# A third pair of batch 2 in cluster order, and GpSimd's transfers tied to their slots

## The chip, the cores and the metric

The kernel runs on one core of a Trainium2 chip. The metric is device time in microseconds, the median of several executions; lower is better. Three executions of the kernel before took 944.02, 944.16 and 945.89 us, so its time is 944.16 us. The core's engines run side by side, each with its own instruction queue in order: TensorE (PE, matmuls), VectorE (DVE), ScalarE (ACT), GpSimd (POOL) and SyncE (SP, which here only starts transfers). They meet through semaphores.

## The reference, cut to what matters

Attention in which a query sees only the keys of its own cluster, and behind it a feed-forward network with a PReLU.

```python
# q, k, v: (4, 8, 768, 64); centroids: (8, 16, 64); scale = 1/8
q_assign = argmax(normalise(q) @ normalise(centroids).T)   # a cluster of 16 per query
k_assign = argmax(normalise(k) @ normalise(centroids).T)
scores = where(q_assign[..., None] == k_assign[..., None, :], scale * q @ k.T, -1e9)
attn = softmax(scores) @ v
x = attn.transpose(0, 2, 1, 3).reshape(3072, 512)
h = x @ w_in                                               # 512 x 2048
out = (maximum(h, 0) + alpha * minimum(h, 0)) @ w_out      # 2048 x 512
```

All inputs are random; all values are 32-bit floats.

## The kernel before

**Tiling.** The 8 heads of each of the 4 batches are taken two at a time: 16 *pairs*, four to a batch, numbered 0 to 15. A pair has 768 tokens, in six chunks of 128 keys. The feed-forward of a batch is done in two halves of 384 tokens, and each half consists of 28 *pieces*: 16 hidden ones (L1055, four matmuls, a copy out of PSUM on ScalarE at L1061, the PReLU's slope on VectorE at L1047) and 12 final ones (L1073, four matmuls; the result is copied by ScalarE at L1079 or added by VectorE at L1081, and stored by SyncE at L1084).

**Two ways to do a pair.** Pairs below `NO` (10 before) are done in two halves of 384 queries. Each half scores all six chunks of keys (L774), takes the exponentials on ScalarE (L795), masks them on VectorE by comparing clusters (`mask`, L815), adds them up (L825) and weighs the values (L929). Pairs from `NO` on are done *in cluster order*: the rows of q, k and v are first sorted by cluster, so that each chunk of keys scores only a window of queries (224, 384, 320, 320, 384 and 224 columns, 1856 of 4608 for a head), and the results are sorted back.

**What cluster order costs.** VectorE and a few small matmuls compute each row's rank (`order_sims` L572, the scan L586, `order_begins` L598, `order_rows`). Then 24 indirect transfers, started by GpSimd (`order_scatter`, L666), write the rows to a scratch tensor in DRAM. Four of them share one staging tile, which SyncE fills by three transfers (`order_stage`, L652), and GpSimd adds the row numbers to it (L663). There are two staging tiles. `order_load` (SyncE) fetches the sorted rows three or four steps ahead of the pair. After the attention, `weigh_near` (L962) and `normalise_near` make the result; `to_rows` turns it on TensorE (L992) and ScalarE copies it out (L995) into two tiles that every pair uses; twelve indirect transfers by GpSimd (`put_back`, L1000) write it to DRAM in the old order; `fetch_back` (SyncE, L1012) reads it and `turn_back` (VectorE, L1019) puts it into `xT`, the feed-forward's input.

**The order of the work** is written out by hand and the tile framework only adds the waits. The work is a list of *steps*, three to each half pair or whole pair, called a group. Before, batch 2 has steps 48 to 65: the whole pairs 10 and 11 at 48 and 51, then the first halves of 8 and 9 at 54 and 57, then their second halves at 60 and 63. Batch 3 is steps 66 to 77, four whole pairs. In the second part of the kernel, from step 24, a group has 15 *ticks*. The first three score the first three chunks, weigh and normalise the group before, and score the other chunks. The other twelve are *slots*. In each slot, in this order, one small task of the group runs, then up to one scatter (two in the slots of a group's first step) is taken from the deque `sorting` if it holds any, then feed-forward pieces are fed, so that a block's pieces are spread evenly over its slots. Things set by `later(k, ...)` run k ticks on: the put-backs of a pair run one per tick, from 8 to 19 ticks after its normalisation, `fetch_back` in the tick after them and `turn_back` nine ticks later.

The list `feeds` says from which step on a half of a batch is fed: the first half of batch 2 in steps 60 to 65, the second in 66 to 77, and `kept` says how many pieces are left over for the next block. `ORDERS` gives the step at which each sorted pair's loading starts.

**Waits.** Nothing holds GpSimd to its slot but the data: a scatter needs its staging tile and its ranks, a put-back its rows. SyncE is one queue in order, so a stage load that waits for scatters to free its tile holds all that is behind it, the stores and fetches too.

Of the kernel before, what the change touches and what calls it, by code (L numbers as in the profile page):

```python
# [10 lines left out]
FP32 = mybir.dt.float32  # L11
# [12 lines left out]
def kernel(  # L24
# [70 lines left out]
    def later(slots, piece):  # L95
        due.setdefault(now[0] + slots, []).append(piece)
# [5 lines left out]


    pairs = [(b, hp) for b in range(B) for hp in range(NCH)]
    NO = WHOLE * NCH - 2
    NP = len(pairs)
    raw_qk, vts = {}, {}

# [383 lines left out]
    def second_part():  # L492

        first_part.close()
        for name, bufs in (("emore", 1), ("ordc", 1), ("ordp", 1), ("order", NP - NO),
                           ("xmore", 1), ("byrow", 1)):
            sorts[name] = fast.enter_context(tc.tile_pool(name=name, bufs=bufs))
        for i in range(5):
            e_tiles.insert(0, sorts["emore"].tile([P, 2, HS], FP32, name=f"more{i}"))

    def order_constants():

        ordc = sorts["ordc"]
        stage = [ordc.tile([P, NX // PARTS, P], FP32, name=f"stage{i}") for i in range(STAGES)]
        place = ordc.tile([P, HS], U16, name="place")
        nc.gpsimd.iota(place, pattern=[[1, HS]], base=0, channel_multiplier=0)

        number = ordc.tile([P, NX], I32, name="number")
        nc.gpsimd.iota(number, pattern=[[TS, NX]], base=0, channel_multiplier=1)

        kinds = [[[0, P // NC], [1, NC]], [[2, 2], [0, 2], [1, 2], [0, NC]],
                 [[0, 2], [1, 2], [0, Q]]]
        rows, cols = [], ordc.tile([P, 3], FP32, name="cols")
        brief = asg.tile([P, HS], FP32, name="simT")
        assert NX // PARTS > len(kinds)
        own = stage[0][:, 0:len(kinds), :]
        for i, pattern in enumerate(kinds):
            row = (ordc.tile([P, P], FP32, name=f"row{i}") if i else brief[:, 0:P])
            nc.gpsimd.iota(row, pattern=pattern, base=0, channel_multiplier=0,
                           allow_small_or_imprecise_dtypes=True)  # L520
            nc.gpsimd.tensor_tensor(out=own[:, i, :], in0=row, in1=ident, op=ALU.mult)
            rows.append(row)
        same = brief[:, 2 * P:3 * P]
        before, within = rows[1], rows[2]
        shift = ordc.tile([P, 2], FP32, name="shift")

        def columns():
            nc.vector.tensor_reduce(out=cols, in_=own, axis=AX.X, op=ALU.add)
            for t in stage:
                nc.gpsimd.memset(t, 0.0)  # L530

        def sums_before():
            nc.vector.tensor_scalar(out=same, in0=rows[1], scalar1=cols[:, 1:2],
                                    scalar2=None, op0=ALU.is_equal)
            nc.vector.scalar_tensor_tensor(out=before, in0=rows[0], scalar=cols[:, 0:1],
                                           in1=same, op0=ALU.is_gt, op1=ALU.mult)

        def sums_within():  # L540
            nc.vector.scalar_tensor_tensor(out=same, in0=rows[0], scalar=cols[:, 0:1],
                                           in1=same, op0=ALU.is_equal, op1=ALU.mult)
            nc.vector.scalar_tensor_tensor(out=within, in0=rows[2], scalar=cols[:, 2:3],
                                           in1=same, op0=ALU.is_gt, op1=ALU.mult)
            nc.vector.tensor_tensor(out=within, in0=within, in1=before, op=ALU.add)

        def shifts():
            nc.vector.tensor_scalar(out=shift[:, 0:1], in0=cols[:, 2:3], scalar1=-float(HS),  # L550
                                    scalar2=None, op0=ALU.mult)
            nc.vector.tensor_scalar(out=shift[:, 1:2], in0=cols[:, 1:2], scalar1=2.0,
                                    scalar2=float(S), op0=ALU.is_ge, op1=ALU.mult)
            nc.vector.tensor_scalar(out=shift[:, 1:2], in0=shift[:, 1:2], scalar1=-1.0,
                                    scalar2=None, op0=ALU.add)
        for i, piece in enumerate((columns, sums_before, sums_within, shifts)):
            later(5 + i, piece)
        begins = ordc.tile([P, NP - NO], FP32, name="begins")
        sorts.update(stage=stage, number=number, place=place, before=before, within=within,
                     shift=shift, begins=begins)  # L560
# [71 lines left out]
    def order_clusters(n, begin):  # L632
# [9 lines left out]
            nc.vector.tensor_reduce(out=first, in_=begunT, axis=AX.X, op=ALU.add)  # L642
        firsts[n] = first

    def order_stage(n, i):

        b, hp = pairs[n]
        h, part = divmod(i, PARTS)
        head, t = 2 * hp + h, sorts["stage"][i % STAGES]
        rows = slice(part * S // PARTS, (part + 1) * S // PARTS)  # L650
        for src, p0, d0 in ((q, 0, 0), (k, TS, 0), (v, TS, D)):
            nc.sync.dma_start(out=t[p0:p0 + TS, :, d0:d0 + D],  # L652
                              in_=src[b, head, rows].rearrange("(x p) d -> p x d", p=TS))
# [18 lines left out]
    def order_load(n):  # L672
        assert len(scattered[n]) == 2 * NX
        whole = scratch.pop(n)[0]
        found = sorts["order"].tile([P, 2, NJ, 1], I32, name="found")
        for h in range(2):
            r0 = 2 * h * S
            nc.sync.dma_start(out=found[:, h], in_=whole.bitcast(I32)[
                r0:r0 + S, D:D + 1].rearrange("(j p) d -> p j d", p=P))
        orders[n] = found  # L680
        for w in range(2):
            raw = inp.tile([P, 2, NJ, D], FP32, name="qk")
            for h in range(2):
                r0 = (2 * h + w) * S
                for x in range(D // Q):
                    r = h * D + x * Q
                    nc.sync.dma_start(
                        out=raw.rearrange("p h j d -> p (h j d)")[r:r + Q, :].rearrange(
                            "p (t i) -> p t i", i=Q),
                        in_=whole[r0:r0 + S, x * Q:(x + 1) * Q].rearrange(  # L690
                            "(t p) i -> p t i", p=Q))
            raw_qk[n, w] = raw
        vt = vpool.tile([P, 2, NJ, D], FP32, name="vt")
        for h in range(2):
            r0 = (2 * h + 1) * S
            nc.sync.dma_start(out=vt[:, h], in_=whole[r0:r0 + S, D:2 * D].rearrange(
                "(j p) d -> p j d", p=P))
        vts[n] = vt
# [20 lines left out]
    for b in range(B):  # L719
        whole = [n for n in range(b * NCH, (b + 1) * NCH) if n >= NO]  # L720
        rest = [n for n in range(b * NCH, (b + 1) * NCH) if n < NO]
        begun_at.append(len(steps))
        steps += [(n, None, s) for n in whole for s in range(SB)]
        for half in range(2) if rest else ():
            if half:
                begun_at.append(len(steps))
            steps += [(n, half, s) for n in rest for s in range(SB)]
            feeds[len(steps)] = b, half
    begun_at.append(len(steps))
    assert NJ == 6 and GROUP == 2  # L730

# [265 lines left out]

    def put_back(to, place, rows, i):
        j, h = divmod(i, 2)
        nc.gpsimd.indirect_dma_start(  # L1000
            out=to[i],
            out_offset=bass.IndirectOffsetOnAxis(ap=place[:, h, j:j + 1], axis=0),
            in_=rows[j // HJ][:, j % HJ, h * D:(h + 1) * D], in_offset=None, element_offset=h * S * D)

    def fetch_back(n, whole):
# [11 lines left out]
        def turn_back():  # L1017
            for half in range(2):
                nc.vector.transpose(out=x_tile(b, half)[:, hp, :],  # L1019
                                    in_=raw[:, half * HS:(half + 1) * HS])  # L1020
        later(4 if n == NP - 1 else 9, turn_back)

    def x_tile(b, half):
        if (b, half) not in xTs:
# [330 lines left out]
    FREE = SLOTS * SB - 3  # L1355


    ORDERS = [26, 29, 35, 38, 41, 50]
    prep_at, load_at = {}, {}
    for (n, half), u in start_of.items():  # L1360
        def at(step, slot, piece):
            prep_at.setdefault((step, slot), []).append(piece)
        if half is None:
            t = ORDERS[n - NO]
            load_at.setdefault(t, []).append(lambda n=n: load(n))
            for i in range(2):
                at(t + 1, FIRST + i, lambda n=n, i=i: order_features(n, i))
            at(t + 2, 2, lambda n=n: order_sims(n))
            load_at.setdefault(u - (3 if n == NO + 1 else 4), []).append(
                lambda n=n: order_load(n))  # L1370
            at(u - 4, 0, lambda n=n: prep_clusters(n))
            for i in range(2):
# [42 lines left out]
    def feed_block(u):  # L1415
        if u == NS:

            for i, p in ((5, 0), (7, 1)):
                ffn[i] = lambda piece=ffn[i], p=p: (piece(), w_in_sums(p))
            ffn.extend(last_pieces())  # L1420
            return
        ffn.extend(ffn_pieces(*feeds[u]))

    def kept(u):


        return {NS: 12, begun_at[-2]: 8, begun_at[-3]: 2}.get(block_end(u), 0)

    def block_end(u):
        return min(x for x in begun_at if x > u)  # L1430
# [59 lines left out]
    for u in range(TOGETHER, NS + 1):  # L1490
# [54 lines left out]
        for i in slots:  # L1545
# [4 lines left out]
            places = (block_end(u) - block_start(u)) // SB * FREE  # L1550
            pieces = len(ffn) - kept(u) + -whole * (places - 1 - at_slot) // places
            todo.popleft()()
            room = 1 + (s == 0)
            while sorting and room:
                scatters, piece = sorting.popleft()
                piece()
# [229 lines left out]
```

## Time and profile before

| | |
|---|---|
| median of the runs | 944.16 us |
| profiled execution | 985.67 us, its span 983.8 us |
| mean granted TensorE clock in it | 0.982 |
| TensorE busy | 937.1 us, 95% |
| VectorE busy | 664.7 us, 68% |
| GpSimd busy | 286.1 us, 29% |
| ScalarE busy | 251.1 us, 26% |
| 144 scatters (L666) | 150.4 us, 1044 ns each |
| 72 put-backs (L1000) | 70.9 us, 985 ns each |

The profile is of one execution, and that one took longer than the timed ones. Busy time of an engine is the time in which it had at least one instruction under way; a group of rows of one line and form gives its count, busy time and mean duration, then the idle time just before its instructions and what ended most of it ("<-ACT rows L995": a result that line 995 wrote on ScalarE). Starting a transfer on GpSimd shows as a DMA_INDIRECT row; on SyncE (SPq) such rows are the queue's own. A matmul of 32-bit floats shows as two records.

### The profile page before, as it was taken

How to read it: one execution, taken by the hardware profiler on the slowest of the kernel's cores; microseconds unless marked ns; L12 is line 12 of the kernel's file. 1: busy time of each engine (PE TensorE's matmuls, PEld its weight loads, DVE VectorE, ACT ScalarE, POOL GpSimd, SP SyncE). 2: the span in 40 equal slices, each digit the busy share in tenths (PEclk: the TensorE clock that was granted, in tenths of full speed). 3: DMA queues.
4: the chain of work that ended last, by engine and by line, in shares of the span. 5: the costliest groups of instructions: out<-in, count | busy, mean ns of one | idle time of the engine just before them, and what ended most of it. 6: DMA issues, size and time to landing. Idle time of an engine off the chain costs nothing.

```text
span 983.8 us, 11365 instructions
## 1 busy us (share of the span) xinstructions
PE 937.1 (95%) x3995; PEld 502.6 (51%) x3995; DVE 664.7 (68%) x1247; ACT 251.1 (26%) x462; POOL 286.1 (29%) x333
## 2 busy tenths in 40 slices
PE   8999999999997999999994989999999999999997
PEld 5534444454453454444541544545455554556886
DVE  5897789799496677888970946554788636598200
ACT  5674534222121221221210312122222210221000
POOL 2332222110055266631376475000034351000000
PEclk9999999999998999999996899999999999999999
DMA  7442676064012455714822122902031112000000
GB/s 285 134 131 89 138 156 98 12 124 123 0 46 80 106 141 111 141 31 99 143 73 62 33 70 78 115 1 49 22 70 32 32 33 56 1 0 1 22 22 25
DMA packets 209665, 73.35 MB, mean 75 GB/s; under 512 B 194289, under 2 KB 198081, under 8 KB 209601
## 3 DMA queue, kind: packets, MB, share of 16 engines
q1 hardware_dynamic: 201840, 60.35, 28.7%
q0 software_dynamic: 6912, 11.81, 3.7%
q8 instruction: 33, 0.54, 0.2%
q10 hardware_dynamic: 848, 0.39, 0.2%
q14 instruction: 32, 0.25, 0.1%
HBM read 49.89 MB, written 22.28 MB: 73 GB/s over the span
## 4 chain that ended last, share of the span: by engine, by line
PE 85%; DVE 8%; another core or an unknown queue 3%; issue 2%; ACT 0%; DVEq 0%; POOL 0%; POOLq 0%; ACTq 0%
PE fps L1055 25%; PE fps L1073 23%; PE vps L929 7%; PE sps L774 6%; PE sps L1289 4%; PE sps L1233 4%; PE fps L774 3%; PE vps L1289 2%; PE vps L1233 2%; PE fps L1289 1%; PE fps L1233 1%; PE vps L962 1%; PE sps L783 1%; PE mps L962 1%
## 5 line engine op out<-in xcount | busy, mean ns | idle before, releaser
L1055 PE MATMUL fps<-xT,w_in_sb 128*128 128x384 f32 x768 | 260.2, 493 | 7.0 <-issue 5.5
L1073 PE MATMUL fps<-w_out_sb,gT 128*128 128x512 f32 x576 | 256.5, 599 | 4.7 <-issue 3.5
L666 POOL DMA_INDIRECT scratch<-stage,off x144 | 150.4, 1044 | 196.9 <-DVE acc L825 69.2
L1055 PEld LDWEIGHTS fps<-xT,w_in_sb 128*128 128x128 f32 x768 | 143.8, 191 | 111.0 <-issue 13.1
L1073 PEld LDWEIGHTS fps<-w_out_sb,gT 128*128 128x128 f32 x576 | 107.9, 191 | 138.8 <-issue 129.6
L1000 POOL DMA_INDIRECT back<-rows,found x72 | 70.9, 985 | 175.8 <-ACT rows L995 155.3
L1061 ACT COPY gT<-fps 128x384 f32<-128x384 f32 x96 | 46.0, 479 | 231.6 <-PE fps L1055 193.6
L1047 DVE SCALAR_TENSOR_TENSOR gT<-gT,alpha 128x384 f32<-128x384 f32 x96 | 61.1, 648 | 57.3 <-ACT gT L1061 43.1
L774 PE MATMUL sps<-qkT 64*128 64x384 f32 (+1 forms) x480 | 89.4, 487 | 0.0
L795 ACT ACTIVATE E<-sps 128x768 f32<-128x768 f32 (+1 forms) x78 | 58.1, 789 | 78.1 <-PE sps L783 38.4
L897 DVE RECIPROCAL inverses<-mps 64x12 f32<-64x12 f32 (+1 forms) x44 | 11.0, 249 | 82.2 <-remote 40.5
L774 PEld LDWEIGHTS sps<-qkT 64*128 64x128 f32 x480 | 43.5, 186 | 40.0 <-issue 14.8
L815 DVE SCALAR_TENSOR_TENSOR more<-aq,key,more 128x384 f32<-128x384 bf16 (+2 forms) x120 | 63.1, 585 | 1.3 <-ACT more L792 1.1
L929 PE MATMUL vps<-E,vt 128*64 128x384 f32 x316 | 58.6, 495 | 1.4 <-DVE xT L1031 1.4
L815 DVE SCALAR_TENSOR_TENSOR E<-aq,key,E 128x384 f32<-128x384 bf16 (+2 forms) x96 | 50.2, 577 | 3.8 <-ACT E L795 1.6
L825 DVE TENSOR_TENSOR acc<-acc,E 128x768 f32<-128x768 f32 x37 | 35.3, 954 | 14.7 <-ACT E L795 13.6
L271 POOL TENSOR_TENSOR w_in_sb<-w_in_sb,power 128x512 f32<-128x512 f32 x16 | 24.0, 1502 | 69.2 <-DVE w_in_sb L268 69.2
L795 ACT ACTIVATE more<-sps 128x768 f32<-128x768 f32 (+1 forms) x42 | 31.1, 774 | 37.2 <-PE sps L774 33.8
L271 POOL TENSOR_TENSOR w_out_sb<-w_out_sb,power 128x512 f32<-128x512 f32 x16 | 22.9, 1433 | 57.3 <-DVE w_out_sb L268 57.3
L1079 ACT COPY y<-fps 128x512 f32<-128x512 f32 x18 | 10.6, 586 | 105.7 <-PE fps L1073 82.6
L774 PE MATMUL fps<-qkT 64*128 64x384 f32 (+1 forms) x144 | 33.1, 497 | 3.1 <-ACT y L1079 2.9
L1081 DVE TENSOR_TENSOR y<-y,fps 128x512 f32<-128x512 f32 x24 | 16.4, 682 | 26.2 <-PE fps L1073 26.2
(281 smaller groups left out, 1118.9 us busy)
## 6 DMA issues: line engine op xcount, KB each, us to landing
raw<-in_moe_w_in_dram SPq DMA_DIRECT2D x16, 512.0 KB
raw<-in_moe_w_out_dram SPq DMA_DIRECT2D x16, 512.0 KB
out_dram<-y SPq DMA_DIRECT2D x21, 256.0 KB
qk<-in_q_dram SPq DMA_DIRECT2D x48, 96.0 KB
qk<-in_k_dram SPq DMA_DIRECT2D x48, 96.0 KB
qk<-scratch SPq DMA_DIRECT2D x48, 96.0 KB
w_in_kept<-w_in_sb SPq DMA_DIRECT2D x8, 512.0 KB
vt<-in_v_dram SPq DMA_DIRECT2D x10, 384.0 KB
```

The source lines that it names most:

```text
L271: nc.gpsimd.tensor_tensor(out=dst, in0=dst, in1=power[0].bitcast(FP32), op=ALU.mult)
L666: nc.gpsimd.indirect_dma_start(out=scratch[n][1][h * NX + xx], out_offset=bass.IndirectOffsetOnAxis(ap=ranks[n][:, xx, h:h + 1], axis=0), ...
L774: nc.tensor.matmul(out=bank(ps, h, m), lhsT=qkT[r:r + D, S + c * P:S + (c + 1) * P], rhs=qkT[r:r + D, tokens], start=True, stop=not early_ ...
L795: nc.scalar.activation(out=E[:, :, 0:m], in_=ps[:, :, 0:m], func=AF.Exp, scale=SCALE)
L815: nc.vector.scalar_tensor_tensor(out=e, in0=of, scalar=keys[n][:, NJ + c, h:h + 1], in1=e, op0=ALU.is_equal, op1=ALU.mult)
L929: nc.tensor.matmul(out=po[r:r + D, 0:HS], lhsT=vts[n][:, h, c, :], rhs=e[:, h, :], start=(c == 0), stop=(c == NJ - 1))
L1000: nc.gpsimd.indirect_dma_start(out=to[i], out_offset=bass.IndirectOffsetOnAxis(ap=place[:, h, j:j + 1], axis=0), in_=rows[j // HJ][:, j % ...
L1047: nc.vector.scalar_tensor_tensor(out=gs[f], in0=gs[f], scalar=alpha[:, f:f + 1], in1=gs[f], op0=ALU.mult, op1=ALU.max)
L1055: nc.tensor.matmul(out=ps[:, 0:HS], lhsT=w_in_sb[:, c, f * P:(f + 1) * P], rhs=xTs[b, half][:, c, :], start=(c == 0), stop=(c == NCH - 1))
L1073: nc.tensor.matmul(out=ps[:, 0:DM], lhsT=gs[f][:, i * P:(i + 1) * P], rhs=w_out_sb[:, f, :], start=on and f == f0, stop=off and f == f0 + ...
L1233: nc.tensor.matmul(out=bank[to], lhsT=w_in_form(m, x, cc), rhs=rhs[:, cc, :], start=start and cc == 0, stop=cc == KH - 1, skip_group_check ...
L1289: nc.tensor.matmul(out=bank[to], lhsT=g_form(m, x, t), rhs=w_out_form(n, x), start=start and x == 0, stop=x == NQ - 1, skip_group_check=no ...
```

## The change

`NO` becomes 9, so that pair 9 is done in cluster order too, and three of batch 2's four pairs are. Batch 2 now has steps 48 to 62: whole pairs 9, 10 and 11 at 48, 51 and 54, then both halves of pair 8 at 57 and 60. Batch 3 is steps 63 to 74, and there are 75 steps, not 78. Both feed-forward halves of batch 2 are fed from step 63 on, behind its attention; the slots of steps 48 to 62 get the pieces of the second half of batch 1.

GpSimd is tied to the slots: `pace()` has ScalarE write one number into a tile of one element and GpSimd copy that tile. It stands ahead of each put-back and in each slot that takes something from `sorting`. The pool has 8 such tiles.

Around it: the tile `found` (the sorted rows' old places) moves into the tile of the ranks, the pool "order" has one buffer more, `order_load` runs three steps ahead for three pairs and four for the others, `turn_back` comes seven ticks after the fetch, and steps from 45 on may take two scatters in one slot more of a group.

```diff
-    NO = WHOLE * NCH - 2
+    NO = WHOLE * NCH - 3
...
-                           ("xmore", 1), ("byrow", 1)):
+                           ("xmore", 1), ("byrow", 1), ("pace", 8)):
...
+        sorts["paced"] = ordc.tile([1, 1], FP32, name="paced")
...
+    def pace():
+
+        token = sorts["pace"].tile([1, 1], FP32, name="pace")
+        nc.scalar.copy(token, ones[0:1, 0:1])
+        nc.gpsimd.tensor_copy(out=sorts["paced"], in_=token)
+
     def order_stage(n, i):
...
-        found = sorts["order"].tile([P, 2, NJ, 1], I32, name="found")
+        found = ranks[n].rearrange("p x h -> p (x h)")[:, 0:2 * NJ].rearrange(
+            "p (h j d) -> p h j d", h=2, d=1)
...
-            if half:
+            if half and not whole:
                 begun_at.append(len(steps))
             steps += [(n, half, s) for n in rest for s in range(SB)]
-            feeds[len(steps)] = b, half
+            feeds[len(steps)] = [(b, 0), (b, 1)] if whole else [(b, half)]
...
     def put_back(to, place, rows, i):
         j, h = divmod(i, 2)
+        pace()
         nc.gpsimd.indirect_dma_start(
...
-        later(4 if n == NP - 1 else 9, turn_back)
+        later(4 if n == NP - 1 else 7, turn_back)
...
-    ORDERS = [26, 29, 35, 38, 41, 50]
+    ORDERS = [26, 29, 35, 38, 41, 53, 56]
...
-            load_at.setdefault(u - (3 if n == NO + 1 else 4), []).append(
+            load_at.setdefault(u - (3 if n in (NO + 1, NO + 2, NP - 1) else 4), []).append(
                 lambda n=n: order_load(n))
...
-        ffn.extend(ffn_pieces(*feeds[u]))
+        for b, half in feeds[u]:
+            ffn.extend(ffn_pieces(b, half))
...
-        return {NS: 12, begun_at[-2]: 8, begun_at[-3]: 2}.get(block_end(u), 0)
+        return {NS: 12, begun_at[-2]: 2, begun_at[-3]: 2}.get(block_end(u), 0)
...
-            room = 1 + (s == 0)
+            room = 1 + (s == 0 or (u >= NS - 30 and (s, i) == (1, 0)))
+            if room and sorting:
+                pace()
             while sorting and room:
```

## The prediction

> **What bounds the kernel now.** I read the busy times first, then the chain that ended last, the groups of GpSimd, the waits, and last the timeline around 550 to 607 us, where batch 2's two cluster-ordered pairs are put back while pairs of batch 3 are still scattered.
>
> ```profile
> PE 937.1 (95%) x3995; PEld 502.6 (51%) x3995; DVE 664.7 (68%) x1247; ACT 251.1 (26%) x462; POOL 286.1 (29%) x333
> PE 85%; DVE 8%; another core or an unknown queue 3%; issue 2%; ACT 0%; DVEq 0%; POOL 0%; POOLq 0%; ACTq 0%
> ```
>
> TensorE is the bound: busy 95%, with 85% of the chain. What shortens TensorE's work pays in full, unless something holds it up. ScalarE has room, and GpSimd looks idle on average. The average misleads: GpSimd's transfers are crowded into stretches. The groups of GpSimd (count, then busy us and mean ns, then idle before):
>
> ```profile
> L666 POOL DMA_INDIRECT scratch<-stage,off x144 | 150.4, 1044 | 196.9 <-DVE acc L825 69.2 <-DMA stage<-in_v_dram 62.7 <-issue 34.3
> L1000 POOL DMA_INDIRECT back<-rows,found x72 | 70.9, 985 | 175.8 <-ACT rows L995 155.3 <-issue 20.2 <-DMA stage<-in_q_dram 0.3
> L663 POOL COPY stage<-number 64x4 int32<-64x4 int32 x36 | 9.4, 262 | 0.0
> ```
>
> Now the timeline (start, duration, instruction, idle before it). The second half of a pair's rows is ready at 560.97 (first line), but its first put-back runs at 570.38, 9.4 us late, and GpSimd is back to back (0.30 idle) up to the last at 582.56:
>
> ```profile
> 560.49 0.48 ACT L995 COPY rows<-mps 128x384 f32<-128x384 f32 x1
> ...
> 567.42 1.04 POOL L1000 DMA_INDIRECT back<-rows,found  x1 [0.30 <-issue]
> 568.46 0.27 POOL L663 COPY stage<-number 64x4 int32<-64x4 int32 x1
> 569.01 1.06 POOL L666 DMA_INDIRECT scratch<-stage,off  x1 [0.28 <-issue]
> 570.38 0.96 POOL L1000 DMA_INDIRECT back<-rows,found  x1 [0.30 <-issue]
> ...
> 582.56 0.96 POOL L1000 DMA_INDIRECT back<-rows,found  x1 [0.30 <-issue]
> ...
> 606.54 0.98 POOL L666 DMA_INDIRECT scratch<-stage,off  x1 [7.01 <-DMA stage<-in_v_dram]
> ```
>
> So a scatter costs 1.044 + 0.30 = 1.34 us of GpSimd, a put-back 0.985 + 0.30 = 1.29. Here lateness costs TensorE nothing: the one thing that waits for put-backs at once, ScalarE's copy into the rows (L995), lost 3.3 us to them in the whole span.
>
> The profiled execution took 985.67 us, 41.5 over the median. It holds stalls in which TensorE, VectorE, ScalarE and SyncE stand together while GpSimd goes on; the largest is in the waits (us, times, longest):
>
> ```profile
> DVE inverses L897 <- remote: 40.5, 3, 29.9
> ...
> SPq L652 <- DMA scratch<-stage,off: 121.3, 15, 51.4
> ```
>
> These stalls add up to 40 to 47 us, about the whole excess, so I take them to belong to the profiled execution and not to the runs. My sum is a difference between kernels, made on the profile's durations outside the stalls and laid on the median.
>
> **What the Trainium skill says.** "DMA: Bandwidth & Descriptors", section SWDGE vs HWDGE vs iDMA: descriptors of a GpSimd DMA are computed in software on GpSimd itself; SyncE's are not. The trace agrees: each transfer holds GpSimd about 1 us. "SBUF — State Buffer", section A bandwidth-pool intuition that's wrong: such a DMA takes about 620 ns alone and about 3100 ns beside a VectorE copy that locks the shared port. Here the shortest is 0.96 us; the page gives me the ends of a transfer's price. "ScalarE: Activation LUTs", section What ACT_TABLE_LOAD costs: an ACTIVATE takes 186 ns + 0.833 ns per element; this trace's 128x1 ones take 202 and 203 ns.
>
> **The change, part by part.**
>
> (1) Pair 9 goes in cluster order. A half pair's TensorE groups, between 604 and 686 us: scores 5.3 us / 28 = 0.189 each, weighing (5.0 + 4.4) / 52 = 0.181. Two halves are 48 of each: 9.1 + 8.7 = 17.8, and 0.6 for folding sums. A whole pair scores 1856 of 4608 columns. By the spacing of starts its 24 narrower scores take 3.9 us, weighing 3.9, turning to rows 0.65, begins 0.5, sums 0.4, together 9.4; its similarities cost what the other form's do. Saving 18.4 − 9.4 = 9.0. The busy totals of the narrow groups, which count twice where two matmuls overlap, give a smaller saving, 6.5. Spacing is the better measure of what the engine has left for others, so I take **8.5**, with the ends 6.5 and 9.
>
> (2) Feed-forward order. No piece is added or removed: batch 2's two halves (28 pieces each, about 85 us a half) run behind its attention, 28 pieces over 60 slots in steps 48 to 62, then 46 over 48 slots in steps 63 to 74. TensorE's sum is unchanged. VectorE in steps 48 to 62 comes to 127 to 131 us (three ordered groups at 19.7, two half groups at 15.5, feed-forward 13, sorting and preparing the rest) beside 133 of TensorE: covered, with little left. If not covered: 3 to 5 us.
>
> (3) The token. Before each slot's scatters and each put-back, ScalarE writes one number and GpSimd copies it: about 228 tokens (144 slots, 84 put-backs). ScalarE 228 × 0.2 = 46 us on an engine busy 26%: hidden while ScalarE runs ahead of TensorE's need. GpSimd about 0.17 each (below the 0.26 of L663), 39 us. The token lies in a pool of 8 tiles, so ScalarE's token n waits until GpSimd has copied token n − 8. Behind that ScalarE instruction stand the exponentials and the feed-forward's copies out of PSUM, and TensorE waits for those banks. So **GpSimd may be at most eight tokens late before it stops ScalarE and then TensorE**; and it can no longer run scatters ahead of their slot, as it did 10 to 39 us before 553 us. That is new.
>
> (4) GpSimd's demand against TensorE's supply of time, counted from the code by step and slot (58.1 is step 58, slot 1). TensorE's side is the whole or half pair of (1) and the feed-forward pieces of these slots, at 8 × 36.8 / 112 = 2.6 us for a hidden piece (L1055) and 8 × 28.2 / 64 = 3.5 for a final one (L1073); GpSimd's side (12 put-backs per ordered pair from eight ticks after it is normalised; up to one scatter a slot, two in the slots of a group's first step):
> Steps 52.4 to 55.3: 12 put-backs (15.5) + 15 scatters (20.1) + 4 copies and 24 tokens (5.6) = 41 us, while TensorE's work there is 28.
> 55.4 to 58.0: 12 put-backs, 1 scatter, 13 tokens = 19 against 23.
> 58.1 to 62.4: 12 put-backs, 24 scatters, 6 copies, 33 tokens = 55 against 41.
> Together 116 against 92, excess 24. Further, pair 14's first stage loads are queued on SyncE behind pair 10's fetch back, in the same tick, which waits for the last put-back: from the timeline 1.6 + 2.8 + 1.9 + about 2.5 = 8.7 us of idle GpSimd. Against it eight tokens of lateness, about 8 × 1.5 = 12 us, are free. ScalarE's stall: 24 + (0 to 9) − 12 = 12 to 21; part of it falls where TensorE has feed-forward ends that VectorE adds up. I take **15**, bounds 0 (a transfer of about 1.0 us with its token, where demand meets supply) and 28.
>
> (5) Turning back 7 ticks after the fetch instead of 9. Fetches that come late make VectorE wait 3 to 7 us at step 56 and 62, mostly inside (4)'s stall: **1**, bounds 0 to 4. The positions kept in the ranks' tile, the later load by one step: SyncE's, off the path, 0 to 1.
>
> Sum: −8.5 + 15 + 1 = +7.5; 944.2 + 7.5 = 951.7, say **951**.
>
> **Rivals.**
> A. GpSimd keeps up, and ScalarE is never held. For it: GpSimd was 29% busy, and unprofiled transfers may be shorter than 1.04 (the page's 0.62). Against: 0.30 between transfers and the crowd at 553 to 583. It decides at a period below about 1.1 us, token included. Then 944.2 − 8.5 + 1 = **937**, faster (935 to 942).
> B. VectorE becomes the bound in steps 48 to 62: 129 of 133 busy, and groups of steps 57 to 59 need 31.7 of VectorE beside 27.6. Without (4): −8.5 + 4 = **940**, faster.
> C. The profile's stalls are in the runs too and the tokens take them away, by keeping GpSimd from running ahead: 944 − 8.5 − 10 or more, **925 to 930**. Against: median and profile differ by just their sum.
> D. The token stall is just as large as the gain: 942.5 to 946, no change, at a period near 1.2 us.
>
> **How the numbers follow.** A difference under 0.2% (1.9 us) is what a measurement of this kernel can't tell from none. Held by GpSimd: 0.57, own range 946.5 to 961. D: 0.07. A 0.20, B 0.13, C 0.03: faster 0.36. The range reaches from 936 (A and B nearly whole; below it lie C and A's best, 0.08) to 961 (15 + 9 of stall, above it 0.1).
>
> **What would show it.** Right: ScalarE rows of a 1x1 copy waiting for GpSimd in steps 52 to 63, TensorE gaps there of 12 us or more in sum, GpSimd back to back, and the group of weighing (L929) down by 48 records. Wrong: no ScalarE wait on GpSimd's copy, TensorE without gaps between steps 48 and 63; or a transfer period well under 1.2 us. If the runs held the profiled stalls, or if GpSimd's wait for a token cost more than 0.3 us each, my sum is wrong from its base.

## The result, and the profile after

The changed kernel takes 973.34 us (970.51 to 974.19), the kernel before beside it 945.02 us: a ratio of 1.0297, 95% interval 1.0279 to 1.0315. It is **slower by 28.3 us**, where +7.5 was forecast (951, range 936 to 961). The direction was right; the size was wrong by nearly four times.

The page of the changed kernel (busy time and share; then the chain that ended last; then groups with count, busy us and mean ns, and idle before). Its profiled execution took 972.51 us, like the others:

```profile
PE 928.9 (96%) x3963; PEld 499.2 (51%) x3963; DVE 658.5 (68%) x1246; ACT 267.0 (28%) x679; POOL 393.3 (41%) x598
...
PE 76%; POOL 8%; DVE 6%; issue 3%; DMA 3%; SPq 2%; ACT 1%; POOLq 0%; ACTq 0%; DVEq 0%
...
L673 POOL DMA_INDIRECT scratch<-stage,off x168 | 180.1, 1072 | 74.4 <-issue 30.7
...
L650 POOL COPY paced<-pace 1x1 f32<-1x1 f32 x223 | 59.1, 265 | 161.9 <-ACT pace L649 160.3
...
L1009 POOL DMA_INDIRECT back<-rows,off x84 | 87.3, 1039 | 19.9 <-issue 14.8
```

In the profile ahead of the prediction GpSimd had no part in the chain and TensorE had 85%; now GpSimd holds 8% and TensorE 76%. The waits of the changed kernel (us, times, longest) name the hold that the prediction expected:

```profile
POOL paced L650 <- ACT pace L649: 160.3, 31, 57.8
...
ACT pace L649 <- POOL paced L650: 69.5, 45, 5.6
...
DVE xT L1028 <- DMA qk<-back: 22.6, 3, 8.1
```

In the first line GpSimd waits for its slot, which is what the tokens are for. In the second ScalarE waits for GpSimd's copy of the token eight before, 69.5 us in 45 places, 41 of them between 481 and 606 us. The third is VectorE waiting in order for a fetch that comes late.

The profile before, as the prediction had it, held stops of all engines. So the kernel before was run again for a trace without them.

> The kernel before, unaltered, for a trace of it from the same chip. Theory 4 (GpSimd, not ScalarE's hold, is what batch 2 is bound by once a third pair is in cluster order; the wait that passes it on to TensorE is whichever comes first: the token, the rows' tiles, the fetch back): where it takes about 944 us, its trace has no stop of all engines, and TensorE's gaps between 20 and 900 us are under 12 us in sum.

It took 944.51 us (ratio 0.9997, 0.9989 to 1.0005). The profiled execution, 947.29 us with a span of 944.9, holds no stop, and its gaps between 20 and 900 us come to 9 us; it is the one to compare. Its page and chain, and then its window of 485 to 625 us (us; busy PE, PEld, DVE, ACT, POOL; granted TensorE clock; DMA share; GB/s):

```profile
PE 926.9 (98%) x3995; PEld 498.5 (53%) x3995; DVE 662.2 (70%) x1247; ACT 249.5 (26%) x462; POOL 298.1 (32%) x333
PE 88%; DVE 5%; DMA 2%; SPq 2%; issue 1%; POOL 1%; ACT 0%; DVEq 0%; POOLq 0%; ACTq 0%
```

```profile
485.00:625.00 140.00, 138.41 (x505) 69.07 (x504) 93.18 (x165) 31.10 (x60) 80.58 (x85) 0.99 0.35 73
```

The same view of the changed kernel, in stages and in one:

```profile
485.00:505.00 20.00, 14.80 (x49) 7.16 (x49) 9.79 (x19) 5.19 (x19) 15.63 (x27) 0.83 0.38 89
505.00:525.00 20.00, 12.83 (x60) 6.05 (x57) 15.35 (x32) 4.30 (x17) 15.91 (x27) 0.83 0.30 60
...
565.00:585.00 20.00, 11.98 (x50) 5.54 (x50) 11.23 (x23) 7.17 (x23) 17.82 (x29) 0.74 0.57 106
...
485.00:625.00 140.00, 113.48 (x429) 55.52 (x428) 93.60 (x178) 35.33 (x124) 107.96 (x172) 0.90 0.44 90
```

Read two things. TensorE stands for 140 − 113.5 = 26.5 us of this stretch, against 1.6 before: 25 us of new gaps. And while it is busy its granted clock is 0.90, not 0.99: 113.5 × 0.10 = 11.3 us of its busy time is lost to the clock, against 1.4, so 10 more. With 7 us of matmuls saved (below), −7 + 25 + 10 = +28, close to the measured 28.3 (the spans of these two profiled executions differ by 25.7, since the one before is a little above its median). The gaps and the slow clock lie in batch 2's block: outside it TensorE's idle time in the two kernels agrees within 1.3 us.

### The profile page after: what moved, and what is told of

It reads as the page before. It is cut to its first block, busy times and chain, and to the rows that moved or that the text cites. A ratio compares the mean times of both kernels' runs of the same rounds, so it can differ in the third digit from the quotient of the medians.

```text
span 970.6 us, 12039 instructions
## 1 busy us (share of the span) xinstructions
PE 928.9 (96%) x3963; PEld 499.2 (51%) x3963; DVE 658.5 (68%) x1246; ACT 267.0 (28%) x679; POOL 393.3 (41%) x598
## 4 chain that ended last, share of the span: by engine, by line
PE 76%; POOL 8%; DVE 6%; issue 3%; DMA 3%; SPq 2%; ACT 1%; POOLq 0%; ACTq 0%; DVEq 0%
PE fps L1082 22%; PE fps L1064 20%; PE vps L937 6%; PE sps L782 5%; PE sps L1298 4%; PE sps L1242 4%; POOL back L1009 3%; POOL scratch L673 3%; PE vps L1298 2%; PE vps L1242 2%; PE fps L782 2%; POOL paced L650 2%; PE fps L1242 1%; PE fps L1298 1%; DMA stage<-in_v_dram 1%
## 5 line engine op out<-in xcount | busy, mean ns | idle before, releaser
L673 POOL DMA_INDIRECT scratch<-stage,off x168 | 180.1, 1072 | 74.4 <-issue 30.7
L650 POOL COPY paced<-pace 1x1 f32<-1x1 f32 x223 | 59.1, 265 | 161.9 <-ACT pace L649 160.3
L1009 POOL DMA_INDIRECT back<-rows,off x84 | 87.3, 1039 | 19.9 <-issue 14.8
L782 PE MATMUL sps<-qkT 64*128 64x384 f32 (+1 forms) x464 | 85.7, 485 | 0.0
L803 ACT ACTIVATE E<-sps 128x768 f32<-128x768 f32 (+1 forms) x76 | 56.1, 785 | 59.2 <-PE sps L791 39.0
L823 DVE SCALAR_TENSOR_TENSOR more<-aq,key,more 128x384 f32<-128x384 bf16 (+2 forms) x116 | 60.7, 580 | 1.3 <-ACT more L800 0.8
L937 PE MATMUL vps<-E,vt 128*64 128x384 f32 x292 | 54.6, 498 | 1.4 <-DVE xT L1040 1.4
L649 ACT COPY pace<-ones 1x1 f32<-1x1 f32 x223 | 33.6, 185 | 69.6 <-POOL paced L650 69.5
L271 POOL TENSOR_TENSOR w_in_sb<-w_in_sb,power 128x512 f32<-128x512 f32 x16 | 23.7, 1482 | 69.5 <-DVE w_in_sb L268 69.5
L823 DVE SCALAR_TENSOR_TENSOR E<-aq,key,E 128x384 f32<-128x384 bf16 (+2 forms) x88 | 45.3, 570 | 0.7 <-ACT E L800 0.6
L833 DVE TENSOR_TENSOR acc<-acc,E 128x768 f32<-128x768 f32 x35 | 33.3, 951 | 14.6 <-ACT E L803 13.6
```

What stands on the lines that cost most here:

```text
L650: nc.gpsimd.tensor_copy(out=sorts["paced"], in_=token)
L673: nc.gpsimd.indirect_dma_start(out=scratch[n][1][h * NX + xx], out_offset=bass.IndirectOffsetOnAxis(ap=ranks[n][:, xx, h:h + 1], axis=0), ...
L782: nc.tensor.matmul(out=bank(ps, h, m), lhsT=qkT[r:r + D, S + c * P:S + (c + 1) * P], rhs=qkT[r:r + D, tokens], start=True, stop=not early_ ...
L803: nc.scalar.activation(out=E[:, :, 0:m], in_=ps[:, :, 0:m], func=AF.Exp, scale=SCALE)
L823: nc.vector.scalar_tensor_tensor(out=e, in0=of, scalar=keys[n][:, NJ + c, h:h + 1], in1=e, op0=ALU.is_equal, op1=ALU.mult)
L937: nc.tensor.matmul(out=po[r:r + D, 0:HS], lhsT=vts[n][:, h, c, :], rhs=e[:, h, :], start=(c == 0), stop=(c == NJ - 1))
```

## The experiments

The theories are these. *1*: the window of eight tokens stops ScalarE and so TensorE, as forecast. *2*: GpSimd's lateness reaches TensorE anyway, by rows that are free late and fetches that come late. *3*: the tokens' own instructions, and that GpSimd may no longer run ahead, cost most. *4*, formed after the first results and a sharper form of 2: once a third pair is in cluster order GpSimd bounds batch 2's block, and whichever wait comes first passes that on.

The kernel before was measured beside each run and took 944.1 to 945.0 us. In three sets it took 998 to 1012 us, because there the other engines stop now and then while GpSimd sends; those six runs (the first five and the last in order of time) are kept apart, under "Where the engines stop".

**No tokens.** The two calls of `pace()` are left out; nothing holds GpSimd to its slot.

```diff
-        pace()
         nc.gpsimd.indirect_dma_start(
...
-            if room and sorting:
-                pace()
```

> The changed kernel without tokens, again, since the chips differ. Where the kernel before takes about 944 us (no stop of the other engines beside GpSimd's bursts), theory 1 gives 934 to 940 us: the third pair alone is worth its matmuls, and the tokens cost the rest. Where the kernel before takes 990 us or more, the other engines stop beside GpSimd's bursts, and with 12 more put-backs and 24 more scatters it is 10 to 30 us slower than before.

953.63 us beside 944.62, ratio 1.0091 (1.0075 to 1.0108). Without a token the kernel is still 9 us slower than before, where 934 to 940 was expected, so theory 1 is not the whole cause. But taking all tokens away does win 973.3 − 953.6 = 19.7 us; the next two runs divide that. In the timeline of this run ScalarE waits again, for something else:

```profile
512.50 0.48 ACT L1003 COPY rows<-mps 128x384 f32<-128x384 f32 x1 [11.42 <-DMA back<-rows,off]
```

The put-backs of the pair before still read the rows' tile, and the copy into that tile stands for 11.4 us. TensorE has a gap of 8.9 us behind it.

**A window of 128 tokens.** One tile of 128 numbers in turn replaces the pool of 8 tiles.

```diff
-        token = sorts["pace"].tile([1, 1], FP32, name="pace")
+        token = sorts["tokens"][:, i:i + 1]      # i counts up, modulo 128
```

> The changed kernel with 128 tokens, again. Where the kernel before takes about 944 us, theory 1 gives 936 to 944 us (ScalarE is never held by GpSimd's copy). Where it takes 990 us or more, the time is within 6 us of the changed kernel's, 984 us: without the hold, GpSimd falls behind and then runs back to back, and the other engines stop beside it instead.

966.77 us beside 944.62, ratio 1.0223 (1.0203 to 1.0244): 6.6 us below the changed kernel, not 30. The hold at eight is real but small, and theory 1 falls as the main cause: once it is gone, ScalarE waits 16.6 us for the rows' tile instead.

**GpSimd's copy alone**, read from a constant, with no number of ScalarE's.

```diff
-        token = sorts["pace"].tile([1, 1], FP32, name="pace")
-        nc.scalar.copy(token, ones[0:1, 0:1])
-        nc.gpsimd.tensor_copy(out=sorts["paced"], in_=token)
+        nc.gpsimd.tensor_copy(out=sorts["paced"], in_=ones[0:1, 0:1])
```

> The changed kernel with GpSimd's copy kept in each place but read from a constant, so that no number of ScalarE's is waited for and nothing holds ScalarE. It parts the 13 us between no tokens (953.6 us) and a window of 128 tokens (966.8 us). If GpSimd's copies cost it by their own time (223 at 0.04 to 0.2 us more a transfer): 960 to 967 us where the kernel before takes about 944. If the loss is that GpSimd may not run ahead of the slot: 953 to 957 us.

962.71 us beside 944.82, ratio 1.0195. GpSimd's copies cost 962.7 − 953.6 = 9.1 us, writing the slot's number on ScalarE and waiting for it 966.8 − 962.7 = 4.1, the hold at eight 973.3 − 966.8 = 6.5. These are the steps in this one order; in another they could divide otherwise. So theory 3 holds for the larger part of what the tokens cost, though not for the whole loss. A copy takes the place of most of the pause between two transfers, as GpSimd's timeline of the changed kernel shows (a scatter, the copy, the next scatter: 1.31 us from start to start, against 1.26 without a copy), so most copies add little more than 0.05 us:

```profile
495.25 0.97 POOL L673 DMA_INDIRECT scratch<-stage,off  x1 [0.16 <-issue]
496.23 0.18 POOL L650 COPY paced<-pace 1x1 f32<-1x1 f32 x1
496.56 0.97 POOL L673 DMA_INDIRECT scratch<-stage,off  x1 [0.16 <-issue]
```

Where a staging copy comes between, the token's copy adds some 0.1 us (0.59 us from the end of one transfer to the start of the next, against 0.48). How the 9.1 us divide between the two cases was not measured.

**The rows in the pair's own tile**, without tokens. The two shared tiles for the put-backs go; the rows are written over the pair's values, which are free after its weighing.

```diff
-        rows = [sorts["byrow"].tile([P, HJ, P], FP32, name=f"rows{i}") for i in range(2)]
+        flat = vts.pop(n).rearrange("p h j d -> p (h j d)")
+        rows = [flat[:, i * HS:(i + 1) * HS].rearrange("p (j d) -> p j d", j=HJ)
+                for i in range(2)]
```

> The changed kernel without tokens, and each pair's rows for the put-backs kept in that pair's own tile of values (free after its weighing) in place of two tiles that all pairs share: ScalarE's copy of the rows no longer waits for the put-backs of the pair before (11.4 us of waiting, and a TensorE gap of 8.9 us behind it, in the run without tokens that took 953.6 us). If that wait is a cause of its own: 938 to 945 us on such a chip. Theory 4: the wait moves on to VectorE's turning back, which waits for the fetch, and the time is 947 to 953 us. On a chip where the kernel before takes 990 us or more, no forecast but that it stays above 985 us.

953.94 us beside 944.82: no gain at all, as theory 4 had it, and 1 us above its figures. ScalarE's wait is gone and TensorE's gap has moved to 521 us:

```profile
532.79 2.29 PE L970 MATMUL mps<-more,vt 128*64 128x384 f32 x8 [11.29 <-DVE inverses L905]
```

The inverses stand on VectorE behind a turning back that waits for the fetch, that is, for the same put-backs. **With a third staging tile** (`STAGES = 3`) in the room that the rows left:

> The same with three staging tiles, not two, in the room that the rows left: GpSimd no longer idles for 7 to 8 us at a time for stage loads that stand on SyncE behind the loads of sorted pairs (at 476, 550 us in the run without tokens). Theory 4, with SyncE's queue as what makes GpSimd late: 5 us or more under the run with rows in the values' tile alone. If GpSimd's own instructions alone make it late: within 2 us of it.

948.07 us, ratio 1.0034 (1.0020 to 1.0048), 5.9 us less (one further execution on record took 4656 us and is left out of the ratio; why is not known). So part of GpSimd's lateness comes from waiting for its staging tiles, which SyncE fills in order between the loads of sorted pairs. **Then the turning back of pairs 9 and 10 set later**, 13 ticks behind the fetch and not 7:

> The run with rows in the values' tile and three stages (948.1 us), and the turning back of pairs 9 and 10 set 13 ticks behind their fetch, not 7. Theory 4 (GpSimd late, and the first wait in order passes it on; here VectorE's for the fetch back, a TensorE gap of 4.9 us at 521 us and the slow clock behind it): 941 to 944 us, faster than the kernel before (944.8). If the wait only moves on once more: 946 us or more.

950.79 us beside 944.13: no gain, 2.7 us more. The wait moved on once more, to feed-forward pieces: two TensorE gaps, 1.6 and 4.7 us at 594 and 599 us, behind a VectorE addition (`PE fps L1065 <- DVE y L1091`) that stands in order behind a wait of 17.5 us for a fetch. So three waits have now carried the lateness, ScalarE's for its token, ScalarE's for the rows' tile and VectorE's for the fetch, the last of them by two ways.

**Feed order alone.** The kernel before, ten pairs in halves, no tokens; only batch 2's feed-forward is put behind its attention.

```diff
-            if half:
+            if half and not whole:
                 begun_at.append(len(steps))
-            feeds[len(steps)] = b, half
+            feeds[len(steps)] = [(b, 0), (b, 1)] if whole else [(b, half)]
...
-        return {NS: 12, begun_at[-2]: 8, begun_at[-3]: 2}.get(block_end(u), 0)
+        return {NS: 12, begun_at[-2]: 2, begun_at[-3]: 2}.get(block_end(u), 0)
```

> The kernel before (ten pairs in halves, no tokens) with batch 2's feed-forward behind its attention alone: 28 pieces over steps 48 to 65, 46 over steps 66 to 77. The prediction costed this at nothing. If it is right: 944 to 946 us. If the thinner feed-forward in batch 2 leaves TensorE less to do beside GpSimd's and VectorE's crowd: 948 us or more.

968.07 us beside 944.13, ratio 1.0251 (1.0236 to 1.0266): **24 us for the part that was forecast at nothing**. The timeline of VectorE in that run shows how:

```profile
540.61 0.57 DVE L477 STREAM_TRANSPOSE aq<-every 128x384 bf16<-128x384 bf16 x1
560.20 1.04 DVE L1019 STREAM_TRANSPOSE xT<-qk 128x384 f32<-128x384 f32 x2 [19.02 <-DMA qk<-back]
```

With 28 pieces in the block instead of 48, TensorE comes to each slot sooner, and the transfers that belong to the slots before it are not done. VectorE stands 19 us for a fetch that needs the last put-back; TensorE stands 3.0 us behind that, and 6.5 us more at 571 us while VectorE catches up. But VectorE is also short of time by itself, before any late fetch. Here is 465 to 505 us in this run, then in the kernel before (columns as above):

```profile
465.00:485.00 20.00, 16.59 (x95) 9.06 (x92) 19.68 (x41) 4.87 (x11) 14.04 (x17) 1.00 0.56 116
485.00:505.00 20.00, 16.89 (x94) 9.62 (x92) 19.22 (x40) 6.62 (x13) 15.47 (x18) 1.00 0.20 59
```

```profile
465.00:505.00 40.00, 37.93 (x162) 19.27 (x161) 34.98 (x69) 8.58 (x19) 28.05 (x32) 1.00 0.42 98
```

VectorE is busy 38.9 of the 40 us, and TensorE stands for 6.5 us against 2.1, most of these gaps ending on a result of VectorE. So what a thin block uncovers is VectorE's crowd as well as GpSimd's, and it does so with two pairs in cluster order: theory 4 needs no third pair. TensorE's missing pieces come later, in a block where no other engine has much to do.

**The other way round: more feed-forward in that block.** Six more pieces of batch 1 are left over for steps 48 to 62.

```diff
-        return {NS: 12, begun_at[-2]: 2, begun_at[-3]: 2}.get(block_end(u), 0)
+        return {NS: 12, begun_at[-2]: 2, begun_at[-3]: 8}.get(block_end(u), 0)
```

In the changed kernel, tokens and all:

> The changed kernel itself, tokens and all, with 8 pieces left over for steps 48 to 62, not 2. If the thinning is the larger part of what it loses, beside the tokens: 960 to 968 us where the kernel before takes 944. If the tokens' hold sets the pace of the block whatever TensorE has: within 2 us of 973.

957.94 us beside 944.61, ratio 1.0138 (1.0117 to 1.0159): **15.4 us faster than the changed kernel**, and 2 below its figures, for moving some 18 us of TensorE work from one place to another and nothing else. Its window, to be read beside the changed kernel's, has 9.9 us of gaps and not 26.5, and a better clock:

```profile
485.00:625.00 140.00, 130.06 (x490) 66.35 (x490) 100.84 (x191) 38.31 (x133) 108.90 (x175) 0.95 0.43 91
```

In the run with three staging tiles and no tokens:

> The run without tokens, rows in the values' tile, three stages (948.1 us), with 8 pieces of batch 1's feed-forward, not 2, left over for steps 48 to 62: six pieces, 18 us of TensorE work, move from steps 36 to 47, where VectorE is busy 85% and TensorE all the time. If batch 2's block is too thin: 4 us or more faster, 938 to 944 us, and so faster than both kernels. If only the order of waits in it counts: 947 to 950 us.

944.64 us beside 944.61, ratio 0.9998 (0.9990 to 1.0006): no difference from the kernel before, so the gain over 948.1 is 3.4 us and the forecast of 4 or more missed by little. Its window:

```profile
485.00:625.00 140.00, 135.34 (x520) 69.38 (x518) 102.09 (x195) 28.97 (x60) 99.15 (x107) 0.99 0.48 101
```

Gaps are down to 4.7 us and the clock is back at 0.99. A gap of 2.9 us at 421 us is new, in the block that gave the pieces. Moving twelve:

> The same with 14 pieces left over: 36 us of TensorE work moved. Steps 36 to 47 then hold about 104 us of TensorE work beside about 120 of VectorE, so they become too thin themselves: slower than with 8, 943 to 960 us.

950.74 us, ratio 1.0062: now that block is the thin one (TensorE busy 72.1 of the 80 us from 360 to 440, VectorE 75.8).

**Three gaps**, to price a gap by itself. In the kernel before, ScalarE repeats a copy out of PSUM 20 times at one hidden piece in each of three halves.

```diff
             gs[f] = gpool.tile([P, HS], FP32, name="gT")
+            for _ in range(20 if (b, half) in ((0, 1), (1, 0), (1, 1)) and f == 5 else 0):
+                nc.scalar.copy(gs[f], ps[:, 0:HS])
```

> The kernel before with twenty more copies on ScalarE (the same copy out of PSUM, repeated) at one hidden piece in each of three halves of the feed-forward, at places with no other wait: TensorE waits some 5 us three times. If a gap costs its own length: the time grows by the sum of the three gaps. If TensorE's clock is granted at half for a while behind a gap, as the changed kernel's windows show it: by 2 to 3 us more for each.

975.37 us beside 944.13: +31.2 us. The gaps in its trace are 8.2, 6.7 and 9.0 us, 24.0 in sum; the other 7.3 us are 2.4 for each gap on average. TensorE's busy time agrees: 933.8 us against 926.9 for the same matmuls. The windows behind the first one (columns as above) show where they go:

```profile
246.50:250.00 3.50, 3.50 (x6) 1.98 (x7) 1.95 (x3) 0.29 (x1) 0.00 (x0) 0.50 0.00 0
250.00:254.00 4.00, 4.00 (x16) 1.50 (x15) 1.72 (x3) 0.48 (x1) 0.00 (x0) 0.83 0.01 4
254.00:258.00 4.00, 4.00 (x10) 1.73 (x10) 4.00 (x8) 0.00 (x0) 0.00 (x0) 1.00 0.00 0
```

TensorE is busy without a pause, at half clock for 3.5 us and for part of the next 4: 3.5 × 0.5 + 4 × 0.17 = 2.4 us. Worked out in the same way, the second gap costs 3.7 us and the third 2.3, so 2.4 is a rough price.

**Where the engines stop.** In these runs the kernel before took 1011.72 us (first four) and 997.72 us (the fifth).

> The changed kernel, but ScalarE's token waits for GpSimd's copy of the token 128 before it, not 8 (one tile of 128 numbers in place of a pool of 8 tiles). Theory 1 (the window of eight tokens stops ScalarE and so TensorE): ScalarE's 69.5 us of waiting for GpSimd's copy go, TensorE's gaps between 482 and 616 us fall from 28 to under 8 us, and the time is 936 to 944 us. Theory 2 (GpSimd's lateness itself reaches TensorE, through rows that are free late and fetches that come late): ScalarE's wait goes, but VectorE and TensorE wait for the fetch back and the rows instead, and the time stays above 958 us.

987.88 us, ratio 0.9739. 

> The changed kernel with 16 tiles in the token's pool, not 8. Theory 1: eight more tokens of lateness at 1.3 us each, about 10 us, are free at each of the crowded stretches, which hold ScalarE at about 482 to 520, 528 to 538, 566 to 577 and 589 to 606 us: the time falls to 950 to 960 us, between the changed kernel's and that of a window of 128. Theory 2: no more than 4 us below the changed kernel.

986.89 us, ratio 0.9726. These two, and the next, were forecast for a base of 944; on this one they say little of the window, since 16 and 128 tokens take the same time.

> The changed kernel without any token: the three whole pairs in batch 2 and the feed-forward behind its attention stay, and GpSimd starts a transfer as soon as its data are there. Theory 1: 934 to 940 us (944.2 less 8.5 us of matmuls, and a few us of waits for fetches), a little under the window of 128, since GpSimd may run ahead of its slots again. Theory 2: above 958 us, as GpSimd has the same transfers to make.

1035.28 us, ratio 1.0192 (1.0121 to 1.0264).

> The kernel before with the tokens alone (8 tiles), ahead of each put-back and in each slot that takes something from the deque; ten pairs in halves as before. Theory 1: here too two pairs are put back while others are scattered, so ScalarE is held, but for a shorter time: 946 to 958 us. Theory 3 (the tokens' own instructions and the end of running ahead cost most of the 28 us, the third pair little): 960 us or more.

965.78 us, ratio 0.9528 (0.9464 to 0.9592): on this base the tokens alone, in the kernel before, gain 46 us. On the base of 944 us this version was not run.

> The changed kernel itself, unaltered, beside the kernel before on one chip. In the first experiments the kernel before took 1012 us, not 944. If the chip there stops the other engines whenever GpSimd sends its transfers back to back (theory C of the prediction), then on such a chip the changed kernel gains: 970 to 985 us beside about 1010. If the chips differ by a factor that all kernels share, the changed kernel is slower by 3% wherever it runs.

983.97 us beside 997.72, ratio 0.9948 (0.9916 to 0.9981): here the changed kernel is the faster one. A last run without tokens, with three stages and 6 pieces left over, met such a place too:

> As the run with 8 pieces left over (944.6 us), with 6, so that the block ahead loses less, and the turning back of pairs 9 and 10 nine ticks behind the fetch, as before the change. If the gap in the block ahead goes and batch 2's block stays full: 940 to 943.5 us, faster than both kernels. If the two blocks only trade: 944 to 947 us.

1052.55 us beside 999.67, ratio 1.0584: whether it beats 944 where no stop occurs is not known. Of all versions tried, none is shown to be faster than the kernel before at 944 us.

## Why the prediction was wrong, step by step

**(1) The third pair: right.** 48 records of weighing are gone, as forecast (432 against 480). Where gaps and slow clock are nearly equal, TensorE's busy time is 919.9 us (without tokens, 8 pieces left over) against 926.9: 7.0 us saved, within 6.5 to 9.

**(2) The feed order: the step that failed most.** The prediction said that TensorE's sum is unchanged and that VectorE is covered, and put it at nothing. The sum is unchanged, but the order alone costs 24 us in the kernel before, and giving six pieces back wins 15.4 of the changed kernel's 28.3. The working in (4) used the thin supply (92 us of TensorE beside 116 of GpSimd) as a given and never asked what had made it thin. In the kernel before, batch 2's block had 24 put-backs and 63 scatters beside 48 pieces in 18 steps; now it has 36 and 57 beside 28 pieces in 15. The runs without tokens show the size of the error: there the forecast's other terms make −8.5 + 1 = −7.5, and the measured difference is +9.0, so 16.5 of the 21 us by which the forecast was off are there without any token. How they divide between the feed order and the third pair's own transfers was not measured, since no run had the third pair with the old feed order.

**(3) and (4) The tokens: right in kind, wrong in place and share.** ScalarE does wait for GpSimd's copies, TensorE behind it. All tokens together cost 19.7 us, where 15 was forecast, but mostly not by the hold, so that the two figures are near each other is luck. The hold at eight tokens, the prediction's likeliest cause, is worth only 6.5 us: taken away, GpSimd's lateness reaches TensorE by the rows' tile, then by the turning back, then by the feed-forward's additions. The prediction saw the first of these in the profile before (3.3 us) and passed over it, and put the second at 1 us; in the run without tokens they cost gaps of 8.9 and 3.2 us. It also let GpSimd come to step 52.4 on time. It came late: ScalarE is held for 3.0 us at 463 us and again and again from 481 us on, before the first put-back of pair 9 at 497.9. Just before, stage loads queued on SyncE behind the loads of a sorted pair and of another pair's rows had left GpSimd idle for 7.0 us:

```profile
463.85 0.97 POOL L673 DMA_INDIRECT scratch<-stage,off  x1 [7.00 <-DMA stage<-in_v_dram]
```

Such idling was counted once, at step 58. The token's copy takes 0.18 us as a rule, as estimated, but 0.265 on average, 59 us in sum where 39 was put down; part of it fits into the pause between transfers.

So the term of gaps, 15 + 1 in the forecast, measured 25.

**A term was missing: TensorE's clock.** Behind a gap of 5 to 9 us TensorE runs at half clock for some microseconds, about 2.4 us lost a gap by the experiment, and 10 us in the changed kernel. The profile before showed it (0.5 behind its stops), and the prediction laid it aside with them. The Trainium skill, "TensorE: Matmul & The Clock Gate", section HAM oscillation — how this bites in real kernels, says that waits between bursts throttle TensorE again, so that what follows starts at half rate; this case's 0.50 behind each gap agrees.

**Rivals.** A (GpSimd keeps up, 937) fell: no version without tokens came under 944.6. B named VectorE's crowd in steps 48 to 62 at up to 5 us; in the changed kernel it was not separated from GpSimd's lateness, since VectorE's longest waits there are for GpSimd's put-backs, but with the feed order alone it shows: VectorE is full from 465 to 505 us. C was wrong where the result was measured, since the kernel before has no stops there, and right in kind where they occur: the changed kernel is 0.5% faster there.

**The stops.** The prediction took them to belong to the profiled execution. Going by the times, they do not: where the kernel before takes 998 to 1012 us timed executions must have them too, and elsewhere they have none. What decides between the two is open. The chip's number alone does not: it is the same for the set at 1012 us and for the later run of the kernel before at 944.5.

## What to carry to other kernels

Before moving work off a stretch of the bounding engine, ask which other engines' deadlines run on its clock there: the moved work was their cover, and a neutral sum over the kernel says nothing about it. When an engine is late, taking away the wait that shows it only uncovers the next; give it less to do there, or more time. In a kernel like this one, price a gap of some 7 us on TensorE at its length and 2 to 4 us for the clock behind it.

## What the runs showed of the hardware

Two things were not expected. A gap on TensorE costs more than itself, as above, and it need not be long: in the kernel before, behind one of 1.6 us that ends at 518.6 us, the granted clock is 0.50 from 520 to 522 us and 0.83 in the next 2. And while GpSimd sends indirect transfers back to back, all other engines can stop with no dependency of the program between them. The run without tokens that took 1035 us shows it most plainly (TensorE, VectorE, ScalarE, and then GpSimd at its steady 1.26 us a transfer; start, us, idle before; "remote" is a releaser that the profile can't name):

```profile
313.58 4.21 PE L1063 MATMUL fps<-xT,w_in_sb 128*128 128x384 f32 x6 [17.23 <-ACT more L800]
...
313.00 0.56 DVE L1039 TENSOR_TENSOR xT<-vps,rd 128x384 f32<-128x384 f32 x1 [17.40 <-remote]
...
313.04 0.87 ACT L800 ACTIVATE more<-fps 128x384 f32<-128x384 f32 x2 [22.14 <-remote]
...
297.49 0.96 POOL L673 DMA_INDIRECT scratch<-stage,off  x1 [0.30 <-issue]
298.75 0.96 POOL L673 DMA_INDIRECT scratch<-stage,off  x1 [0.30 <-issue]
...
309.70 0.96 POOL L673 DMA_INDIRECT scratch<-stage,off  x1 [0.30 <-issue]
```

The three engines start again within 0.6 us of each other, 2.3 us after GpSimd's last transfer of that burst has ended. At 944 us the same bursts, with the same 0.30 us pauses, run beside full work. With a copy between the transfers the stops cost less, but they do not go: in the same set the changed kernel with 128 tokens takes 987.9 us against 1035.3 without any, and has one of 12.0 us at 617 us. Their cause was not found.
